# A fused attention and maxout kernel: the pieces ahead of its first loop in another written order

## The chip, the cores and the metric

The kernel runs on 1 core of a Trainium2 chip (8 cores in all). The metric is device time in microseconds of one launch, the median of several runs. Profiled executions give, besides, the span of the kernel's own instructions and the time of each of them.

## The reference

```python
# x: (8, 8, 512, 64), state: (8, 8, 32, 64); per batch b and head h:
scores  = x @ state.T / 8;   a  = softmax(scores,  -1);  xread = a  @ state   # 512 rows
scores2 = state @ x.T / 8;   a2 = softmax(scores2, -1);  sread = a2 @ x       # 32 rows
# heads side by side: 8 * (512 + 32) = 4352 rows of 512
h1 = rows @ w1;  h2 = rows @ w2          # (512, 1024) each
out = maximum(h1, h2) @ w_out            # w_out (1024, 512); float32 out
```

## The kernel before

The kernel uses maximum(h1, h2) = relu(rows @ (w1 - w2)) + rows @ w2. So a first layer with the difference `wd` of the two weights, a relu (`r`), and a second layer with `w_out` (`wo`) give one part. The other part is linear, and for it the product `w2 @ w_out` (`wwo`, 512x512) is made once. Since the rows of a batch are a small softmax matrix times 32 states per head, state times `wd` and state times `wwo` are folded into `sw` (per batch), and `at` (the transposed softmax matrix) is multiplied with `sw`.

The work is staged by batch. Batches 2 to 6 are finished by a loop written at the end of the function, batch 7 by a tail. Batches 0 and 1, the making of `wd`, `wo` and `wwo`, and the first steps of batches 2 to 4 lie ahead of the loop. What is recorded there, and in which order, stands in one string, `ORDER`, of short tokens. Each token calls one helper, so its place sets the place of that helper's instructions in the queue of their engine. Nothing is reordered afterwards: every engine takes its own queue strictly from the front, and waits at the front for what it needs.

A token is read so: name and arguments, then `@` the PSUM banks that it writes, or `>` the engine that does it (A is ScalarE, V is VectorE, P is GpSimd). The ones that matter here:

- `ldx.b.g`, `ldS`, `ldw1.k`, `ldw2.k`, `ldwo.q`: loads from HBM, 512 KB each except the small first `ldS`. They are issued on SyncE (the first `ldS` on ScalarE), and each waits only for the landing of a load further ahead, eight semaphores in turn. The pieces of `w_out` come in the order 2, 3, 0, 1, so `ldwo.3` is the second.
- `ce` casts x (tile `xe`), `xt` transposes it on TensorE (L249), `xte` copies it out of PSUM; `cS`, `S`, `Se` do the same for the state into `sbd`. `sc`, `exp`, `red`, `mul` are the scores and the softmax (`e`, `a`), `at` its transpose on TensorE (L291) and `ate` the copy. `srw` and `swre` make the state read of a batch.
- `cw2.k` casts a quarter of w2, `w2.k` transposes it on TensorE (L548), `w2e.k` copies it to `w2m`. `cwo.q` casts a quarter of w_out into `wo`.
- `ww.i.q` adds the quarter q of `w_out` to `wwo`'s block i: two matmuls 128x512 (L606). `ww.i.q` needs `cwo.q`. `wwe` copies the finished block.
- `sub.k.h` makes a half quarter of `wd` (L560); `sw.b.z` multiplies state with it (L352), `swe` casts the result out of PSUM; `l1.b.f` is the first layer (L375) and `re.b.f` its relu.
- `p1` to `p7`, `k`, `v`, `rs`, `wt`, `dif` are the second layer of batches 0 and 1 (a Strassen-like scheme of seven products, 8 matmuls 128x256 each, L426); `mS` and `Sd` mask the later batches' state and transpose it by DMA into `sbd` (L222, L228).
- `fill.k@bank` is one matmul of a zero tile `wz` with itself into a bank (L575): 256 columns wide, or 512 where k is 100 or more. Its result is never read. There are 27 of them.

```python
    for tok in ORDER.split():                       # L645
        name, _, at_ = tok.partition("@")
        name, _, eng = name.partition(">")
        ...
        if w[0] in mms:
            done[name] = mms[w[0]](*arg)
```

Of the kernel before, what the change touches and what calls it, by code (L numbers as in the profile page):

```python
# [20 lines left out]
CHUNKS = [[(0, 512), (512, 1024)], [(0, 512), (512, 1024)]]  # L21

ORDER = """
ldx.0.0 ldS.0.2 fill.10@0 ldx.0.1 fill.109@1 ldx.1.1 fill.114@0 fill.11@1 ldx.1.0 fill.110@0 ldw2.2 fill.100@1
fill.9@0 ldw2.3 fill.111@1 ldwo.2 fill.0@0 fill.5@1 fill.101@0 ldw1.3 ce.0.1>A ce.0.0>V ldwo.3 xt.0.0@0 cS.0.2>V
ldw1.2 fill.106@1 xte.0.0>V fill.105@2 ce.0.3>P ce.0.2>A ldw2.1 S.0.2@1 xt.0.1@2 ldw2.0 Se.0.2.1>A Se.0.2.0>V sc.0.0@1
xte.0.1>V fill.13@0 ldwo.0 fill.6@3 ce.1.2>P exp.0.0>A fill.115@4 fill.108@3 sc.0.1@4 ce.1.3>V ldwo.1 red.0.0>V
exp.0.1>A xt.1.1@3 ce.1.0>A ce.1.1>P srw.0@4,1 xte.1.1>V ldw1.0 mul.0.0>P swre.0.0>A red.0.1>V sc.1.1@3 xt.1.0@2
cw2.2>P exp.1.1>A ldw1.1 fill.15@4 fill.107@0 xte.1.0>V fill.1@4 swre.0.1>A fill.2@3 fill.14@0 fill.3@4 fill.112@3
cw2.3>A red.1.1>V mul.0.1>P fill.102@4 fill.7@3 ldx.2.0 fill.4@2 mul.1.1>V w2.3@2 cwo.2>A w2.2@3 w2e.3>V sc.1.0@4  # L30
at.0.0@0 at.0.1@1 exp.1.0>A w2e.2>V ww.3.2@2 ldx.2.1 ww.2.2@4 red.1.0>V sub.3.1>P ate.0.0>A srw.1@3,5 ate.0.1>A
mul.1.0>V cwo.3>A ww.0.2@1 sub.3.0>V at.1.0@0 at.1.1@6 swre.1.0>A ww.1.2@7 sub.2.0>V ate.1.1>A ldS.2.8 ww.3.3@2
ww.1.3@7 sub.2.1>V ate.1.0>A ww.0.3@1 swre.1.1>A sw.1.1@0,6 sw.0.1@5,3 swe.1.1.0>A swe.1.1.1>V ww.2.3@4 swe.0.1.0>A
swe.0.1.1>V l1.1.5@6 cw2.1>P srp.0>P srp.1>P l1.1.7@0 cw2.0>A re.1.5>V l1.0.7@3 w2.1@5 re.1.7>V re.0.7>A w2.0@6 w2e.1>V cwo.0>A
l1.0.5@3 l1.1.6@0 w2e.0>V l1.1.4@5 cwo.1>A ww.2.0@4 re.0.5>V ww.1.0@7 re.1.4>A ww.2.1@4 sub.0.0>V ww.1.1@7 re.1.6>A
sub.0.1>V ww.3.0@2 wwe.2>A ww.0.1@1 sub.1.1>V ww.3.1@2 wwe.1>A ww.0.0@1 sub.1.0>V wwe.3>A l1.0.4@7 wwe.0>A cb.2.0>P
sw.0.0@2,4 re.0.4>V wt.0>P sw.1.0@0,5 swe.0.0.0>A swe.0.0.1>V sw.0.w@1,3 sw.1.w@7,6 cb.2.1>P swe.1.0.0>A swe.1.0.1>V xtd.2 wt.1>P
p2.1@2 l1.0.6@4 swe.0.w.0>A re.0.6>V l1.0.3@0 l1.0.2@5 swe.0.w.1>A re.0.3>V swe.1.w.0>V mS.1>A
l1.0.1@4 l1.0.0@1 p2.0@3 swe.1.w.1>V mS.0>A Sd dif.0>P re.0.2>V re.0.1>A re.0.0>A p2o.0
l1.1.0@7 l1.1.1@6 l1.1.2@0 l1.1.3@5 re.1.0>V re.1.1>A re.1.2>A rs.0.0>V rs.0.1>V re.1.3>A  # L40
p2o.1 ldx.4.1 ldx.3.0 ldx.4.0 ldx.3.1
p1.0@1 k0.0>A p1.1@4 rs.0.2>V wt.2>V v00.0 p6.0 rs.0.3>V k0.1>A k1.0>A p5.0@7 wt.3>V v00.1 rs.1.0>V k2.0>A
sc.2.0@6 exp.2.0>A sc.2.1@0 exp.2.1>A sw.2.0@5,3 red.2.0>V mul.2.0>P red.2.1>V swe.2.0.0>A swe.2.0.1>A ce.2.0>A ce.2.1>A ce.2.2>A ce.2.3>A
p7.0 o7.0 v11.0 rs.1.1>V mul.2.1>P p3.0 o3.0 rs.1.2>V atd.2 sw.2.w@6,2 swe.2.w.0>A v01.0 swe.2.w.1>A
p4.0 o4.0 rs.1.3>V ce.3.0>P ce.3.1>P cb.3.0>P ce.3.2>P ce.3.3>P cb.3.1>P v10.0>A store.0 xtd.3 dif.1>P
sr.2@0 p6.1 k1.1>A sw.2.1@5,3 sre.2>V swe.2.1.0>A swe.2.1.1>V p5.1@7 k2.1>A
p7.1 o7.1 v11.1 p3.1 o3.1 v01.1 srt.2@0 srte.2>A p4.1 o4.1 v10.1>A ldx.5.0 ldx.5.1
"""

LATE = 2  # L50
# [851 lines left out]
```

## Time and profile before

| | |
|---|---|
| time of 3 runs | 144.94, 145.07, 145.07 us, median 145.07 |
| the profiled execution | 144.88 us, of which the kernel's span is 143.1 us |
| busy in the span | PE (TensorE) 94%, DVE (VectorE) 76%, ACT (ScalarE) 61%, POOL (GpSimd) 50% |
| HBM | 15.20 MB read, 8.91 MB written |
| granted TensorE clock | 0.996, mean over the span |

The profiled execution is 0.19 us below the median of the runs. The 1.8 us between its time and its span lie outside the instructions. In the profile's rows, PE is a matmul and PEld a weight load, L606 is line 606 of the kernel before, and a name such as `wo<-big` says which tile is written from which. A matmul's duration contains a tail in which the next one already runs, so the pace of a group is read from the chain that ended last, where such tails do not count twice.

### The profile page before, as it was taken

How to read it: one execution, taken by the hardware profiler on the slowest of the kernel's cores; microseconds unless marked ns; L12 is line 12 of the kernel's file. 1: busy time of each engine (PE TensorE's matmuls, PEld its weight loads, DVE VectorE, ACT ScalarE, POOL GpSimd, SP SyncE). 2: the span in 40 equal slices, each digit the busy share in tenths (PEclk: the TensorE clock that was granted, in tenths of full speed). 3: DMA queues.
4: the chain of work that ended last, by engine and by line, in shares of the span. 5: the costliest groups of instructions: out<-in, count | busy, mean ns of one | idle time of the engine just before them, and what ended most of it. 6: DMA issues, size and time to landing. Idle time of an engine off the chain costs nothing.

```text
span 143.1 us, 3680 instructions
## 1 busy us (share of the span) xinstructions
PE 134.7 (94%) x1448; PEld 95.4 (67%) x1458; DVE 108.3 (76%) x197; ACT 86.9 (61%) x168; POOL 72.1 (50%) x99
## 2 busy tenths in 40 slices
PE   6889989999999999999999999999999999999980
PEld 2467725456787776786778477747876786788860
DVE  3488959868999938997899799669948997847420
ACT  4367589895689535855682769086726855753220
POOL 4147326099009993399269908971990464200000
PEclk9999999999999999999999999999999999999998
DMA  3999999945997979949995999759137042502073
GB/s 112 342 366 392 384 386 386 343 83 93 196 343 230 286 180 249 236 42 293 242 386 109 212 355 195 160 213 211 35 65 293 2 58 82 234 5 73 9 248 119
DMA packets 36452, 29.50 MB, mean 206 GB/s; under 512 B 22608, under 2 KB 32336, under 8 KB 35536
## 3 DMA queue, kind: packets, MB, share of 16 engines
q1 hardware_dynamic: 36160, 29.10, 70.8%
q8 instruction: 12, 0.20, 0.6%
q10 hardware_dynamic: 272, 0.13, 0.3%
q14 instruction: 8, 0.07, 0.1%
HBM read 15.20 MB, written 8.91 MB: 169 GB/s over the span
## 4 chain that ended last, share of the span: by engine, by line
PE 83%; DMA 11%; ACT 1%; issue 1%; DVE 0%; SPq 0%; DVEq 0%
PE bank L426 36%; PE bank L375 19%; PE bank L432 10%; DMA big<-in_moe_w_out_dram 8%; PE bank L352 5%; DMA big<-in_x_dram 4%; PE bank L606 3%; PE bank L473 2%; PE bank L515 2%; PE bank L264 2%; PE bank L304 2%; PE bank L513 1%; ACT wo L102 1%; PE bank L548 1%; PE bank L336 0%
## 5 line engine op out<-in xcount | busy, mean ns | idle before, releaser
L102 ACT COPY big<-bank 128x512 f32<-128x512 f32 (+2 forms) x40 | 21.9, 551 | 16.6 <-PE bank L426 8.4
L280 POOL TENSOR_TENSOR a<-e,er 128x512 bf16<-128x512 bf16 x14 | 16.7, 1209 | 29.5 <-ACT e L272 18.0
L370 DVE TENSOR_SCALAR r<-bank 128x512 bf16<-128x512 f32 x32 | 21.9, 690 | 11.7 <-PE bank L375 10.6
L375 PE MATMUL bank<-at,sw 128*128 128x512 bf16 x120 | 29.1, 379 | 0.6 <-DVE sw L104 0.2
L426 PEld LDWEIGHTS <-big 128*128 128x128 bf16 x256 | 23.9, 98 | 6.3 <-DVE er L277 2.1
L426 PE MATMUL bank<-big,big 128*128 128x256 bf16 x192 | 23.1, 273 | 0.1
L102 ACT CAST sw<-bank 128x512 bf16<-128x512 f32 x36 | 20.1, 608 | 3.2 <-PE bank L352 3.2
L375 PEld LDWEIGHTS <-sw 128*128 128x128 bf16 x128 | 12.2, 98 | 13.5 <-ACT sw L102 0.5
L368 ACT ACTIVATE r<-bank 128x512 bf16<-128x512 f32 x32 | 18.3, 597 | 4.9 <-PE bank L375 4.7
L426 PEld LDWEIGHTS <-r 128*128 128x128 bf16 x192 | 18.2, 98 | 3.8 <-issue 0.5
L402 DVE TENSOR_TENSOR big<-bank,big 128x512 f32<-128x512 f32 (+1 forms) x25 | 16.4, 660 | 5.4 <-PE bank L432 5.4
L106 POOL CAST xe<-big 128x512 bf16<-128x512 f32 x23 | 16.5, 749 | 6.1 <-DMA big<-in_x_dram 6.1
L426 PE MATMUL bank<-wo,r 128*128 128x256 bf16 x128 | 16.3, 273 | 0.0
L102 ACT COPY sread_t<-bank 128x128 bf16<-128x128 bf16 x8 | 3.2, 472 | 18.7 <-PE bank L336 15.5
L106 POOL CAST xb<-big 128x1024 bf16<-128x1024 f32 x12 | 12.2, 1035 | 4.7 <-DMA big<-in_x_dram 4.7
L432 PE MATMUL bank<-sw,at 128*128 128x256 bf16 x96 | 14.4, 273 | 0.0
L432 PEld LDWEIGHTS <-at 128*128 128x128 bf16 x128 | 12.5, 98 | 1.7
L402 DVE TENSOR_TENSOR big<-r 128x1024 bf16<-128x1024 bf16 x16 | 12.6, 788 | 0.6
L276 DVE TENSOR_REDUCE sums<-e 128x16 f32<-128x512 bf16 x16 | 10.6, 660 | 0.3 <-ACT e L272 0.2
L272 ACT ACTIVATE e<-bank 128x512 bf16<-128x512 f32 x16 | 8.9, 601 | 1.3 <-PE bank L264 1.3
L402 POOL TENSOR_TENSOR big<-sw 128x512 bf16<-128x512 bf16 x8 | 9.2, 1151 | 0.9 <-POOL a L280 0.9
L104 DVE CAST sw<-bank 128x512 bf16<-128x512 f32 x12 | 7.9, 679 | 0.6 <-PE bank L352 0.6
(100 smaller groups left out, 188.7 us busy)
## 6 DMA issues: line engine op xcount, KB each, us to landing
big<-in_x_dram SPq DMA_DIRECT2D x14, 512.0 KB, 6.2
out_dram<-big SPq DMA_DIRECT2D x7, 1024.0 KB, 5.3
big<-in_moe_w_dram SPq DMA_DIRECT2D x8, 512.0 KB, 12.0
big<-in_moe_w_out_dram SPq DMA_DIRECT2D x4, 512.0 KB, 11.6
big<-in_x_dram SPq DMA_DIRECT2D x1, 1024.0 KB, 6.9
out_dram<-big SPq DMA_DIRECT2D x4, 256.0 KB, 2.6
sf<-in_state_dram SPq DMA_DIRECT2D x1, 384.0 KB, 10.4
out_dram<-w2m SPq DMA_DIRECT2D x2, 128.0 KB, 2.5
```

The costliest lines, as they stand in the source:

```text
L102: nc.scalar.copy(o, i)
L104: nc.vector.tensor_copy(o, i)
L106: nc.gpsimd.tensor_copy(o, i)
L272: nc.scalar.activation(out=e_view(e_s[b % 2], hh).rearrange("p (g c) i n -> p g c (i n)", g=2), in_=p.rearrange("p (c g m) -> p g c m", c= ...
L276: nc.vector.tensor_reduce(es_all[:, b, hh], e_view(e_s[b % 2], hh), axis=AXX, op=ALU.add)
L280: (nc.gpsimd if eng == "P" else nc.vector).tensor_mul(e_view(a_s[b % 2], hh), e_view(e_s[b % 2], hh), er_s[b % 2][:, hh].unsqueeze(3).to_b ...
L368: nc.scalar.activation(out=o, in_=p, func=ACTF.Relu)
L370: nc.vector.tensor_scalar(o, p, scalar1=0.0, scalar2=None, op0=ALU.max)
L375: nc.tensor.matmul(p, sw_s[b % 3][:, g, f * 128:(f + 1) * 128], at_s[b % 3][:, g].rearrange("p c t -> p (c t)"), start=(g == 0), stop=(g = ...
L402: (nc.gpsimd if eng == "P" else nc.vector).tensor_tensor(o, i0, i1, op=op)
L426: nc.tensor.matmul(pv[c], lhs[:, f, 128 * c:128 * c + 128], rhs[:, f, :], start=first and f == 0 and (c == 0 or pv.split), stop=False, ski ...
L432: nc.tensor.matmul(pv[c], at_s[b % 3][:, g, 2 * i + c, :], rhs[:, g, :], start=False, stop=False, skip_group_check=True)
```

## The change

Only the string `ORDER` is another one, and it is one line shorter, so that every later line has a number one lower (L606 is L605 in the kernel after). The tokens of the loads stand in the same order; the number of zero products is the same, 27; the loop and the tail are the same. Other than that nearly every token up to the first instructions of batch 2 has another place, and several have another engine or bank. First and last of it:

```diff
 ORDER = """
-ldx.0.0 ldS.0.2 fill.10@0 ldx.0.1 fill.109@1 ldx.1.1 fill.114@0 fill.11@1 ldx.1.0 fill.110@0 ldw2.2 fill.100@1
...
+fill.115@3 fill.10@6 fill.15@3 fill.100@7 fill.114@5 fill.1@2 fill.107@0 fill.112@4 fill.108@0 fill.9@5 fill.111@3
+fill.106@2 fill.5@7 ldx.0.0 ce.0.1>P ldS.0.2 cS.0.2>P ce.0.0>A fill.105@2 S.0.2@4 Se.0.2.1>V ldx.0.1 ce.0.2>V ce.0.3>A
...
```

Thirteen zero products (8 of 512 columns, 5 of 256) stand ahead of TensorE's first real work, where 11 stood before (6 and 5).

The first place is TensorE's queue around the first product that needs the piece `ldwo.3`. In the kernel before, with the rows that only repeat left out:

```order
L606 MATMUL bank_65<-wo_77,w2m_80 128x512
...
L606 MATMUL bank_67<-wo_77,w2m_80 128x512
...
L606 MATMUL bank_64<-wo_77,w2m_80 128x512
...
L291 MATMUL bank_63<-ident_71,a_94 128x128
...
L291 MATMUL bank_69<-ident_71,a_94 128x128
...
L606 MATMUL bank_70<-wo_77,w2m_80 128x512
...
L606 MATMUL bank_65<-wo_77,w2m_80 128x512
...
L352 MATMUL bank_63<-wd_75,sbd_74 32x512
```

These are `ww.3.2`, `ww.2.2`, `ww.0.2`, `at.1.0`, `at.1.1`, `ww.1.2`, then `ww.3.3`, the first that needs `ldwo.3` (with `ww.1.3` and `ww.0.3` behind it), and `sw.1.1`. The same engine and place in the kernel after:

```order
L605 MATMUL bank_64<-wo_77,w2m_80 128x512
...
L605 MATMUL bank_70<-wo_77,w2m_80 128x512
...
L574 MATMUL bank_63<-wz_73 128x256
...
L290 MATMUL bank_69<-ident_71,a_94 128x128
...
L605 MATMUL bank_64<-wo_77,w2m_80 128x512
...
L605 MATMUL bank_65<-wo_77,w2m_80 128x512
...
L605 MATMUL bank_67<-wo_77,w2m_80 128x512
...
L290 MATMUL bank_66<-ident_71,a_94 128x128
...
L605 MATMUL bank_65<-wo_77,w2m_80 128x512
...
L351 MATMUL bank_63<-wd_75,sbd_74 32x512
```

These are `ww.0.2`, `ww.1.2`, a zero product, `at.1.0`, then `ww.0.3`, now the first that needs `ldwo.3`, and behind it `ww.3.2`, `ww.2.2`, `at.1.1`, `ww.3.3` (and `ww.1.3`), `sw.1.1`. So `ww.3.2`, `ww.2.2` and `at.1.1` (4 matmuls 128x512 and 4 transposes) moved from ahead of that product to behind it.

The second place is ScalarE's queue around the casts of `w_out`. Before:

```order
L102 CAST wo_77<-big_115 128x1024
L272 ACTIVATE e_92<-bank_67 128x8x64
L102 COPY at_99<-bank_63 128x512
L102 COPY at_99<-bank_64 128x512
L102 CAST wo_77<-big_115 128x1024
L102 COPY big_116<-bank_66 128x260
L102 COPY at_100<-bank_69 128x512
```

After:

```order
L271 ACTIVATE e_92<-bank_63 128x8x64
L101 COPY w2m_80<-bank_67 128x4x256
L101 CAST wo_77<-big_115 128x1024
L101 COPY big_116<-bank_69 128x260
L101 CAST wo_77<-big_115 128x1024
L101 COPY at_99<-bank_65 128x512
L101 COPY at_100<-bank_66 128x512
```

The first cast of each fence is `cwo.2`, the second `cwo.3`. The copy `ate.0.1` out of bank 2 (`bank_65`) moved behind `cwo.3`, and `w2e.2` (`w2m`) came onto ScalarE ahead of `cwo.2`.

The third place is ScalarE's queue around the mask of the later batches' state. Before:

```order
L102 CAST sw_102<-bank_64 128x512
L102 CAST sw_102<-bank_66 128x512
L222 ACTIVATE sb_82<-sf_81,mask_83 128x12x64 x2
L368 ACTIVATE r_105<-bank_67 128x512
L368 ACTIVATE r_105<-bank_64 128x512
```

After:

```order
L101 CAST sw_102<-bank_64 128x512
L367 ACTIVATE r_105<-bank_67 128x512
L367 ACTIVATE r_105<-bank_63 128x512
L367 ACTIVATE r_105<-bank_70 128x512
L367 ACTIVATE r_105<-bank_66 128x512
L221 ACTIVATE sb_82<-sf_81,mask_83 128x12x64
```

One of the two masks (`mS.0`) moved behind four relus; the other (`mS.1`) went to GpSimd.

More of the change, by code (lines that the diff above doesn't have):

```diff
@@ L23 @@
 ORDER = """
-ldx.0.0 ldS.0.2 fill.10@0 ldx.0.1 fill.109@1 ldx.1.1 fill.114@0 fill.11@1 ldx.1.0 fill.110@0 ldw2.2 fill.100@1
[L25 to L44, printed above, removed]
@@ L45 @@
-p4.0 o4.0 rs.1.3>V ce.3.0>P ce.3.1>P cb.3.0>P ce.3.2>P ce.3.3>P cb.3.1>P v10.0>A store.0 xtd.3 dif.1>P
-sr.2@0 p6.1 k1.1>A sw.2.1@5,3 sre.2>V swe.2.1.0>A swe.2.1.1>V p5.1@7 k2.1>A
-p7.1 o7.1 v11.1 p3.1 o3.1 v01.1 srt.2@0 srte.2>A p4.1 o4.1 v10.1>A ldx.5.0 ldx.5.1
+fill.115@3 fill.10@6 fill.15@3 fill.100@7 fill.114@5 fill.1@2 fill.107@0 fill.112@4 fill.108@0 fill.9@5 fill.111@3
+fill.106@2 fill.5@7 ldx.0.0 ce.0.1>P ldS.0.2 cS.0.2>P ce.0.0>A fill.105@2 S.0.2@4 Se.0.2.1>V ldx.0.1 ce.0.2>V ce.0.3>A
@@ new lines @@
+ldx.1.1 ldx.1.0 ce.1.0>P ce.1.1>P ldw2.2 ldw2.3 ldwo.2 ldw1.3 ldwo.3 ldw1.2 ldw2.1 ldw2.0 ldwo.0 ldwo.1 ldw1.0 ldw1.1
+ce.1.2>A xt.0.0@5 xte.0.0>V fill.0@2 xt.0.1@1 fill.7@5 fill.3@0 Se.0.2.0>V fill.14@0 sc.0.0@6 ce.1.3>V xte.0.1>V
+fill.110@4 xt.1.1@7 fill.101@1 sc.0.1@4 fill.4@3 fill.13@0 exp.0.0>A red.0.0>V mul.0.0>P xte.1.1>V fill.11@3
+fill.109@6 exp.0.1>A red.0.1>V cw2.2>P cw2.3>V xt.1.0@1 xte.1.0>A srw.0@6,0 swre.0.1>A fill.2@4 sc.1.1@5 exp.1.1>A
+red.1.1>V sc.1.0@0 exp.1.0>A fill.102@5 w2.2@4 mul.0.1>P srw.1@5,0 at.0.0@7 red.1.0>V mul.1.0>V ate.0.0>V swre.1.1>V
@@ new lines @@
+w2e.2>A at.0.1@2 w2.3@4 w2e.3>V cwo.2>A ww.0.2@1 ww.1.2@7 fill.6@0 swre.0.0>A mul.1.1>P at.1.0@6 cwo.3>A ate.0.1>A
+ww.0.3@1 ldx.2.0 ldx.2.1 ldS.2.8 ww.3.2@2 ww.2.2@4 at.1.1@3 ww.3.3@2 ww.1.3@7 ate.1.1>A ate.1.0>V swre.1.0>V sub.2.0>V
+sub.2.1>V sub.3.1>P sub.3.0>P sw.1.1@0,6 swe.1.1.0>A sw.0.1@5,3 ww.2.3@4 swe.1.1.1>V l1.1.7@0 re.1.7>V l1.1.5@6
+swe.0.1.0>A swe.0.1.1>A re.1.5>A cw2.1>P cw2.0>P w2.1@5 w2e.1>V l1.0.7@3 re.0.7>A cwo.0>P w2.0@0 l1.1.4@6 re.1.4>V
+cwo.1>V w2e.0>A l1.1.6@5 ww.2.0@4 l1.0.5@3 re.0.5>A ww.3.0@2 re.1.6>A ww.1.1@7 ww.2.1@4 wwe.2>A ww.1.0@7 ww.3.1@2
@@ new lines @@
+wwe.1>A wwe.3>A wt.0>V sub.0.0>V sub.0.1>V ww.0.0@1 ww.0.1@1 wwe.0>A l1.0.4@6 sub.1.1>V sub.1.0>V sw.0.0@2,4
+swe.0.0.0>A sw.1.0@0,5 swe.1.0.0>A swe.1.0.1>A sw.0.w@1,3 re.0.4>V sw.1.w@7,6 swe.0.0.1>V p2.1@2 l1.0.6@4 l1.0.3@0
+swe.0.w.0>A swe.1.w.1>V re.0.6>A re.0.3>A swe.1.w.0>V swe.0.w.1>V l1.0.1@1 l1.0.0@7 wt.1>V dif.0>V re.0.1>V re.0.0>A
+l1.1.3@5 l1.0.2@3 re.0.2>A mS.0>A wt.2>V rs.0.2>V srp.1>P cb.2.0>P cb.2.1>P ldx.4.1 xtd.2 mS.1>P Sd ldx.3.0 ldx.4.0
+ldx.3.1 l1.1.2@6 l1.1.1@7 re.1.1>A re.1.2>V rs.0.0>V wt.3>V rs.0.1>V p1.0@1 l1.1.0@0 p2.0@3 p2o.0 p5.0@7 re.1.3>A
@@ new lines @@
+re.1.0>A p1.1@4 srp.0>A k0.0>A p6.0 p2o.1 rs.1.0>V v00.0 k0.1>A rs.0.3>V v00.1 k1.0>A sc.2.0@6 exp.2.0>A k2.0>A
+sc.2.1@0 exp.2.1>A sw.2.0@5,3 red.2.0>V mul.2.0>P red.2.1>V swe.2.0.0>A swe.2.0.1>A ce.2.0>A ce.2.1>A ce.2.2>A
+ce.2.3>A p7.0 o7.0 v11.0 rs.1.1>V mul.2.1>P p3.0 o3.0 rs.1.2>V atd.2 sw.2.w@6,2 swe.2.w.0>A v01.0 swe.2.w.1>A p4.0
+o4.0 rs.1.3>V ce.3.0>P ce.3.1>P cb.3.0>P ce.3.2>P ce.3.3>P cb.3.1>P v10.0>A store.0 xtd.3 dif.1>P sr.2@0 p6.1 k1.1>A
+sw.2.1@5,3 sre.2>V swe.2.1.0>A swe.2.1.1>V p5.1@7 k2.1>A p7.1 o7.1 v11.1 p3.1 o3.1 v01.1 srt.2@0 srte.2>A p4.1 o4.1
@@ L48 @@
+v10.1>A ldx.5.0 ldx.5.1
 """
```

## The prediction

> **What bounds the kernel now.** I read the page first, then the chain that ended last, then the timeline at the places where the chain leaves TensorE.
>
> ```profile
> PE 134.7 (94%) x1448; PEld 95.4 (67%) x1458; DVE 108.3 (76%) x197; ACT 86.9 (61%) x168; POOL 72.1 (50%) x99
> PE   6889989999999999999999999999999999999980
> DMA  3999999945997979949995999759137042502073
> PE 83%; DMA 11%; ACT 1%; issue 1%; DVE 0%; SPq 0%; DVEq 0%
> q8 instruction: 12, 0.20, 0.6%
> ```
>
> The second line cuts the span into 40 slices of 3.6 us: TensorE has free tenths in the first six and the last two slices only. The third line says that the DMA engines are full at that time too. The chain has 11% of DMA, and in order of time it shows where.
>
> ```profile
> 6.55 11.23 DMA big<-in_moe_w_out_dram
> 17.79 0.02 issue
> 17.81 1.05 ACT wo L102
> 18.86 0.04 issue
> 18.91 1.46 PE bank L606 x6
> ...
> 23.12 0.89 PE bank L548 x16
> ...
> 25.31 3.45 PE bank L606 x16
> ...
> 37.95 0.87 PE bank L426 x8
> 38.82 0.06 issue
> ```
>
> So what precedes 17.8 us on TensorE does not set the end: the chain goes through the load `ldwo.3`, issued at 6.55 and landed at 17.78, its cast on ScalarE, and the first product that reads it at 18.91. From there to the tail TensorE works with hardly a hole, so work or a wait that is added to it behind 18.91 comes out at the end at full length. The timeline tells what TensorE does around that point.
>
> ```profile
> 17.73 0.59 PE L606 MATMUL bank<-wo,w2m 128*128 128x512 bf16 x2
> 18.91 1.46 PE L606 MATMUL bank<-wo,w2m 128*128 128x512 bf16 x6 [0.58 <-ACT wo L102]
> 20.29 0.67 PE L352 MATMUL bank<-wd,sbd 64*32 64x512 bf16 x16
> 20.89 0.60 PE L606 MATMUL bank<-wo,w2m 128*128 128x512 bf16 x2
> 21.66 0.59 PE L375 MATMUL bank<-at,sw 128*128 128x512 bf16 x2 [0.17 <-DVE sw L104]
> 18.99 1.29 DVE L560 TENSOR_TENSOR wd<-big,big 128x512 bf16<-128x512 f32 x2 [1.22 <-DMA big<-in_moe_w_dram]
> 19.03 1.08 ACT L102 COPY at<-bank 128x512 bf16<-128x512 bf16 x2
> 38.85 1.66 PEld L426 LDWEIGHTS <-big 128*128 128x128 bf16 x16 [0.32 <-DVE big L402]
> ```
>
> The bracket is the idle time and what ended it. Behind 18.91 the holes are 0.17 to 0.3 at 21.66 (the first layer waits for `sw`) and 0.32 at 38.85 (a second-layer product waits for VectorE).
>
> **The change: the first 17.8 us.** Zero products, transposes, casts and the softmax of batches 0 and 1 are in another order there. I cost all of it at nothing, because the load covers it, if TensorE and ScalarE still reach the `ldwo.3` work in time. The rows that limit this:
>
> ```profile
> 9.72 0.61 POOL L106 CAST xe<-big 128x512 bf16<-128x512 f32 x1 [0.88 <-DMA big<-in_x_dram]
> 11.23 0.38 ACT L102 COPY big<-bank 128x260 f32<-128x260 f32 x1 [0.61 <-PE bank L321]
> 11.52 0.60 ACT L272 ACTIVATE e<-bank 128x512 bf16<-128x512 f32 x1
> 12.40 1.05 ACT L102 CAST wb<-big 128x1024 bf16<-128x1024 f32 x1
> ```
>
> The last piece of x lands at 9.7. After, GpSimd casts both its parts, 2 x 0.61, to 10.95; four transposes end near 11.4. Then ScalarE has a row of its own: the copy `xte.1.0` (128x1024 on ScalarE out of PSUM, which the trace doesn't show; between the 0.69 that VectorE takes for it and the 1.05 of the cast, I take 1.05), a state-read copy 0.38, two exponentials 2 x 0.60 with about 0.2 between, `w2e.2` 1.05 and `cwo.2` 1.05, in all to 16.3 or 16.4. A last copy of 0.38 makes it 16.75, and the cast of `ldwo.3` can't begin before 17.8. On TensorE `ww.0.2`, `ww.1.2`, a zero product and `at.1.0` follow `cwo.2`: 0.86 + 0.11 + 0.22, done near 17.6 against 18.9. Both covers have about 1.1 us to spare; an error below that costs nothing, one above it costs its excess. For the same reason 13 zero products ahead of the first transposes where 11 were, a later first score, or a clock that rises earlier or later change nothing.
>
> The loads stand in the same order and wait only for earlier landings, so the landings up to 31 us should be those of before. On SyncE `ldx.4.1` now stands ahead of the DMA transposes and waits for the last subtractions on VectorE; the queue waits there until some 30.3 us and the transposes still go earlier than the 32.9 of before.
>
> **The change: behind the wait.** Both kernels start again at 18.91, but not with the same work left. `ww.3.2`, `ww.2.2` and `at.1.1` were done in the cover of the load and now stand behind `ww.0.3`. A product of 512 columns goes at 3.45 / 16 = 0.216, a transpose at 0.89 / 16 = 0.056 (chain rows above).
>
> - 4 products: +0.86; 4 transposes: +0.22.
> - `ww.3.2` writes bank 2, which ScalarE's copy `ate.0.1` frees, and that copy now stands behind the cast `cwo.3`. The cast begins at 17.81, the next instruction started 0.95 later in before, a copy of this size takes about 0.6 (two in 1.08, overlapped), so the bank is free at 19.36, when `ww.0.3` ends: +0.05. Bounds: 0 and 0.2.
> - `sw.1.1` thus starts at 18.91 + 10 x 0.216 + 0.22 + 0.05 = 21.34 instead of 20.29: +1.05. Its other condition, the subtractions on VectorE (18.99 + 1.29 = 20.28), held it in before for 0.09, and is past now.
> - From `sw.1.1` to the first layer: 21.66 - 20.29 = 1.37 in before, ruled by the eviction of `sw`, with the same tokens between. Unchanged.
> - Later holes that a late TensorE no longer has: 0.32 at 38.85 and bits below 0.1 elsewhere. Bounds: 0 and 0.4 given back. I take 0.3, since the wait is for VectorE, whose queue gets shorter (three relus, an `sw` cast and a `w2m` copy go to ScalarE, two weight sums, a cast and a difference come to it).
> - GpSimd gives two weight sums to VectorE and takes the casts `cw2.0` and `cwo.0`, 1.04 each by the row below, in a stretch where it sat idle for 4 us before the first of its two pieces landed. Their readers, the transposes `w2.0` and the products with that piece, come 1 us later than before. Nothing.
>
> ```profile
> 20.47 1.04 POOL L106 CAST wb<-big 128x1024 bf16<-128x1024 f32 x1 [4.04 <-DMA big<-in_moe_w_dram]
> ```
>
>
> Sum: 1.05 - 0.3 = +0.75; with the bounds of the terms, +0.65 to +1.25. The loop and the tail are the same and have no hole of this size to take it up. The profiled execution is 144.88, so it would be 145.63; on the median of the runs, which is 0.19 higher, 145.07 + 0.75 = 145.8. A measurement of this kernel can tell about 0.2% (0.29 us) from no change.
>
> **The rivals.** *The load lands earlier (faster).* The landing at 17.78 is itself late:
>
> ```profile
> 13.75 1.04 ACT L102 CAST wo<-big 128x1024 bf16<-128x1024 f32 x1 [0.30 <-DMA big<-in_moe_w_out_dram]
> 15.16 1.27 POOL L560 TENSOR_TENSOR wd<-big,big 128x512 bf16<-128x512 f32 x1 [1.73 <-DMA big<-in_moe_w_dram]
> q8 instruction: 1, 0.02, 6.5%
> ```
>
> The first two are readers that wait for pieces landing one after the other, the third is the cast at 17.81 of the chain above: 1.41 apart, then 2.65. The last row is of the DMA view of 15 to 16 us: one packet of instructions, 6.5% of 16 engines for 1 us, so 1.04 us of one engine, and a load is complete when its slowest engine is. This would be TensorE's own next block of instructions, called for when it is so far in its queue. If the changed kernel calls for it over 0.9 us later, `ldwo.3` would land near 16.5, ScalarE would cast it from 16.75, TensorE would go on at 17.85 and be ready for `sw.1.1` at 20.3, as before; with the 0.3 given back, 144.75. Against it: in both programs the same number of instructions (about 260) stands ahead of a point that TensorE passes at 15.5 in before and, by the rows above, between 15.3 and 16.3 now. The Trainium skill, "Runtime: NRT & Kernel Launch", section "Instruction fetch mechanics", has such refills come in 16 KiB blocks of 256 instructions and calls their cost mostly hidden. By that rule the landing would not depend on it and this rival would have no chance; the gap of 2.65 speaks against the rule. Chance 14%.
>
> *The hole is taken up later.* If VectorE and ScalarE are ahead of TensorE by more than I see, and the 0.17 to 0.3 at 21.66 goes as well, the loss is 1.05 - 0.4 - 0.3: 145.4, at the edge of what can be told from no change. Chance 10%.
>
> *The state transpose becomes late.* The third place in the order:
>
> ```profile
> 35.04 1.84 SPq L228 DMA_TRANSPOSE sbd<-sb  x1
> sbd<-sb SPq DMA_TRANSPOSE x1, 4.6
> xt<-xb SPq DMA_TRANSPOSE x6, 5.3
> 40.63 0.63 PE L264 MATMUL bank<-sbd,xt 128*128 128x64 bf16 x16
> 31.52 1.77 ACT L222 ACTIVATE sb<-sf,mask 128x768 bf16<-128x768 f32 x2
> 33.20 1.09 ACT L368 ACTIVATE r<-bank 128x512 bf16<-128x512 f32 x2
> ```
>
> It landed at 39.6, 1.0 ahead of its reader. After, its mask follows the relu of `l1.0.2`, from whose end to the reader TensorE has 3 first-layer blocks (1.29), 5 products of 8 matmuls (4.37) and 8 small matmuls (0.87): 6.5. The path is the tail 0.2, relu 0.55, mask 0.89, transfer 4.6: 6.2. So 0.3 is left. At the 5.3 of a larger transpose (`xt`) it would be 0.4 short: 146.2 to 146.3. Chance 8%.
>
> *The clock falls.* TensorE's hole ahead of 18.91 grows from 0.6 to some 1.3 us.
>
> ```profile
> 1.29 3.81 PE L575 MATMUL bank<-wz 128*128 128x256 bf16 x11 [1.29 <-DVE ones L578]
> 7.23 0.62 PE L249 MATMUL bank<-ident,xe 128*128 128x128 bf16 x8 [0.77 <-ACT xe L102]
> 9.32 0.61 PE L249 MATMUL bank<-ident,xe 128*128 128x128 bf16 x8
> ```
>
> The first 11 zero products (4352 columns) took 0.88 ns a column, twice the 0.42 of later ones: a cold start, 3.8 us long. After the hole of 0.77 eight transposes took 0.62, as those with no hole (0.61). A new cold start would cost half of 3.8, 1.9: 147.7. The Trainium skill, "TensorE: Matmul & The Clock Gate", section "What's actually happening", wants an idle window of about 3.4 us for that. By that rule the hole is too short; the row at 7.23 agrees as far as it goes. Chance 2%.
>
> **How the numbers follow.** Likeliest, 66%: +0.75, 145.8, its own range 145.4 to 146.2. Early load 14%, taken up 10%, late transpose 8%, clock 2%. Faster by over 0.2% (below 144.78): most of the early load, 0.09. Within 0.2% (to 145.36): its rest, 0.05, and half of the taken up, 0.05. Slower: the others, 0.81. The range of 8 in 10 leaves out the early load and the clock, 16%: 145.1 to 146.3.
>
> **What the next profile would show.** Right: the cast of the second `w_out` piece begins again near 17.8; TensorE's hole ahead of 18.9 is over 1 us; behind it ten products of 512 columns and four transposes in place of six, `sw` near 21.3, the first layer near 22.7; no hole at 38.9. Wrong: that cast begins before 17 us, or a new wait for `wo` or `wd` between 21 and 31 us, or the reader of `sbd` near 41.4 waits for a DMA.

## The result and the profile after

The changed kernel takes 146.34 us (median of 6 runs, 145.78 to 146.89), the kernel before beside it 145.00 (6 runs). The ratio is 1.0091 with a 95% interval of 1.0069 to 1.0114: slower by 1.34 us. Forecast was slower by 0.75, at 145.8, with a range up to 146.3. So the sign was right, the size was not, and the time lies just outside the range.

The profiled execution of after is the slowest of its six: 146.89, span 145.0. First the lines of its page: busy times, TensorE's tenths in 40 slices, the chain that ended last, and the queue that brings blocks of instructions.

```profile
PE 135.6 (94%) x1458; PEld 95.5 (66%) x1458; DVE 107.8 (74%) x198; ACT 86.6 (60%) x168; POOL 74.0 (51%) x98
PE   6788869989999999999999999999999999999980
PE 71%; DMA 3%; DVE 2%; ACT 2%; issue 1%; DVEq 0%
q8 instruction: 12, 0.20, 0.6%
```

The totals hardly differ from before. What is new is a 2% of VectorE in the chain (before: 0%), and the 3% of DMA is not the load of before, but a transpose in the loop. The timeline shows the first two of three places; the columns are start, length, engine, line, operation, tiles, count, and in the bracket the idle time ahead and what ended it.

```profile
17.47 0.39 PE L290 MATMUL bank<-ident,a 128*128 128x128 bf16 x4
18.27 1.04 ACT L101 CAST wo<-big 128x1024 bf16<-128x1024 f32 x1 [1.54 <-DMA big<-in_moe_w_out_dram]
19.37 1.51 PE L605 MATMUL bank<-wo,w2m 128*128 128x512 bf16 x6 [1.51 <-ACT wo L101]
20.71 0.39 PE L290 MATMUL bank<-ident,a 128*128 128x128 bf16 x4
20.93 1.03 PE L605 MATMUL bank<-wo,w2m 128*128 128x512 bf16 x4
21.89 0.63 PE L351 MATMUL bank<-wd,sbd 64*32 64x512 bf16 x16
23.01 0.82 PE L374 MATMUL bank<-at,sw 128*128 128x512 bf16 x3
...
30.48 0.40 PE L351 MATMUL bank<-wd,sbd 64*32 64x512 bf16 x4
31.21 0.61 PE L351 MATMUL bank<-wd,sbd 64*32 64x512 bf16 x12 [0.34 <-DVE wd L559]
```

Three places differ. At 19.37 the idle time ahead of the first product with the second piece of `w_out` is 1.51 instead of 0.58, and ten products and four transposes follow it where six products stood; `sw.1.1` starts at 21.89, before at 20.29. And at 31.21 the folding of `wd` for batch 0 (`sw.0.0`) stops in its middle for VectorE. That wait is not in the profile of before, whose row at this place runs through:

```profile
29.12 0.63 PE L352 MATMUL bank<-wd,sbd 64*32 64x512 bf16 x16
```

The chain of after, followed back, starts just ahead of that wait:

```profile
27.22 0.06 DVE big L401
...
27.83 3.34 DVE wd L559 x4
31.17 0.04 issue
31.21 1.04 PE bank L351 x28
...
38.08 0.87 PE bank L425 x8
38.95 0.44 PE bank L431 x4
```

Four subtractions take 3.34 us; in before they took 2.61, and TensorE did not wait for them. At 38.9 the hole of before (0.32, "<-DVE big L402") is gone: two pieces follow each other without a gap.

The third place is in the loop, where the chain goes through a DMA transpose of the softmax matrix (`at<-a`):

```profile
103.92 4.08 DMA at<-a
108.04 3.61 PE bank L374 x16
```

This first-layer group starts 13.60 behind the one at 94.44; in before the same two, at 92.78 and 106.08, are 13.30 apart, and the transpose took 3.4. So 0.30 is lost there, in a loop whose text is the same.

### The profile page after: what moved, and what is told of

Read it like the earlier page. It is cut to its first block, busy times and chain, and to the rows that moved or that the text cites. A ratio compares the mean times of both kernels' runs of the same rounds, so it can differ in the third digit from the quotient of the medians.

```text
span 145.0 us, 3690 instructions
## 1 busy us (share of the span) xinstructions
PE 135.6 (94%) x1458; PEld 95.5 (66%) x1458; DVE 107.8 (74%) x198; ACT 86.6 (60%) x168; POOL 74.0 (51%) x98
## 4 chain that ended last, share of the span: by engine, by line
PE 71%; DMA 3%; DVE 2%; ACT 2%; issue 1%; DVEq 0%
PE bank L425 32%; PE bank L374 17%; PE bank L431 9%; PE bank L351 4%; DMA at<-a 3%; PE bank L472 2%; DVE wd L559 2%; PE bank L514 2%; PE bank L263 2%; PE bank L303 1%; PE bank L512 1%; ACT sw L101 1%; ACT big L101 1%; PE bank L335 0%; ACT w2m L101 0%
## 5 line engine op out<-in xcount | busy, mean ns | idle before, releaser
L279 POOL TENSOR_TENSOR a<-e,er 128x512 bf16<-128x512 bf16 x15 | 18.2, 1228 | 33.2 <-ACT e L271 18.3
L101 ACT COPY big<-bank 128x512 f32<-128x512 f32 (+2 forms) x38 | 21.1, 560 | 15.1 <-PE bank L425 7.1
L374 PE MATMUL bank<-at,sw 128*128 128x512 bf16 x128 | 29.8, 379 | 0.1
L369 DVE TENSOR_SCALAR r<-bank 128x512 bf16<-128x512 f32 x29 | 20.0, 691 | 11.1 <-PE bank L374 10.8
L367 ACT ACTIVATE r<-bank 128x512 bf16<-128x512 f32 x35 | 20.1, 597 | 4.9 <-PE bank L374 4.7
L101 ACT COPY sread_t<-bank 128x128 bf16<-128x128 bf16 x8 | 3.3, 473 | 18.7 <-PE bank L335 15.5
L605 PE MATMUL bank<-wo,w2m 128*128 128x512 bf16 x32 | 7.9, 379 | 1.8 <-ACT wo L101 1.8
L574 PE MATMUL bank<-wz 128*128 128x256 bf16 (+1 forms) x27 | 7.4, 395 | 1.5 <-DVE ones L577 1.3
```

Source lines behind the costliest of these rows:

```text
L101: nc.scalar.copy(o, i)
L279: (nc.gpsimd if eng == "P" else nc.vector).tensor_mul(e_view(a_s[b % 2], hh), e_view(e_s[b % 2], hh), er_s[b % 2][:, hh].unsqueeze(3).to_b ...
L367: nc.scalar.activation(out=o, in_=p, func=ACTF.Relu)
L369: nc.vector.tensor_scalar(o, p, scalar1=0.0, scalar2=None, op0=ALU.max)
L374: nc.tensor.matmul(p, sw_s[b % 3][:, g, f * 128:(f + 1) * 128], at_s[b % 3][:, g].rearrange("p c t -> p (c t)"), start=(g == 0), stop=(g = ...
L605: nc.tensor.matmul(p, w2t[:, f, i, :], wo[:, f, :], start=(first and f % 2 == 0), stop=(last and f % 2 == 1))
```

## The experiments

Two theories. The first: the prediction's step, four products and four transposes behind the load instead of in its cover, is the whole loss, and it is larger than I had it. The second: the step is as large as I had it, and the rest is the new wait at 31.2, made by VectorE's and GpSimd's queues.

### The swap undone: e1_back

The kernel after, with the copy `ate.0.1` ahead of the cast `cwo.3` again, and the four products and four transposes ahead of `ww.0.3`. The diffs from here on show the tokens that move, gathered from their places, not whole lines of the string:

```diff
+ate.0.1>A
 cwo.3>A
-ate.0.1>A
+ww.3.2@2 ww.2.2@4 at.1.1@3
 ww.0.3@1 ldx.2.0 ldx.2.1 ldS.2.8
-ww.3.2@2 ww.2.2@4 at.1.1@3
 ww.3.3@2
```

> The kernel after with three pieces back ahead of the first product that needs the second w_out piece: ww.3.2, ww.2.2, at.1.1, and the copy ate.0.1 ahead of the cast cwo.3. Theory (work that stood under the load's cover stands behind it): TensorE restarts at the same distance from the landing, but sw.1.1 comes about 1.0 us earlier, held then by the subtractions of wd; the wait of 0.5 for wd at 31.2 stays or grows, since VectorE's queue ahead of it ends with a load. In all 0.6 to 1.0 below the kernel after: 145.4 to 145.7. Rival (the loads themselves land later because of the new first microseconds): the landing stays half a microsecond later than in the kernel before and the time stays above 146.0.

Measured: 144.78 (12 runs), ratio to before 0.9994 (0.9973 to 1.0015). The whole loss is gone, more than the 145.4 to 145.7 expected, and the wait for `wd`, expected to stay, is gone too. The rest of the large change cannot be told from nothing. Its timeline:

```profile
18.76 1.46 PE L605 MATMUL bank<-wo,w2m 128*128 128x512 bf16 x6
20.15 0.83 PE L351 MATMUL bank<-wd,sbd 64*32 64x512 bf16 x16
26.30 2.49 DVE L559 TENSOR_TENSOR wd<-big,big 128x512 bf16<-128x512 f32 x4
28.92 0.63 PE L351 MATMUL bank<-wd,sbd 64*32 64x512 bf16 x16
52.05 2.54 PE L374 MATMUL bank<-at,sw 128*128 128x512 bf16 x11
```

TensorE no longer waits at 18.8, nor for `wd`, and reaches the loop's first-layer product at 52.05 (before 52.56, after 54.21). So the swap decides, but this does not yet say by which way: without it the subtractions are also early, end at 28.79, and take 2.49.

### VectorE's queue: e2_wt and e3_both

In the kernel after, VectorE makes a cast of `w_out` (`cwo.1`) and a weight sum (`wt.0`) ahead of the four subtractions; its timeline:

```profile
25.84 0.69 DVE L369 TENSOR_SCALAR r<-bank 128x512 bf16<-128x512 f32 x1 [0.55 <-PE bank L374]
26.45 0.68 DVE L103 CAST wo<-big 128x1024 bf16<-128x1024 f32 x1
27.22 0.69 DVE L401 TENSOR_TENSOR big<-wo 128x1024 bf16<-128x1024 bf16 x1
```

The relu ahead of them waits for TensorE, so a late TensorE makes all of this late. e2_wt has the sum behind the subtractions, and keeps the swap; e3_both has this and the edit of e1_back.

```diff
-wt.0>V
 sub.0.0>V sub.0.1>V
 ...
 sub.1.1>V sub.1.0>V
+wt.0>V
```

> The kernel after with one token moved: the weight sum wt.0 on VectorE behind the four subtractions sub.0.0 to sub.1.0 instead of ahead of them. Theory (VectorE's queue makes sw.0.0 wait): the holes of 0.5 and 0.2 at 31.2 to 32.3 go, 0.5 to 0.7 below the kernel after: 145.7 to 145.8. Rival (TensorE's lateness there is all from the work behind the load, the hole only moves to the first reader of wt.0): no change, 146.3.

> Both edits of the two runs beside it on the kernel after. Theory (two separate losses): the gains add up to 1.1 to 1.5 and the time is that of the kernel before, 145.0 to 145.2. Rival (a third part comes from late landings): 145.4 to 145.7, with the cast of the second w_out piece beginning near 18.3 and not 17.8.

Measured: e2_wt 145.89 (6 runs), ratio 1.0073 (1.0051 to 1.0095); e3_both 144.81 (11 runs), ratio 0.9993 (0.9978 to 1.0008). So by the medians the sum's place is worth 146.34 - 145.89 = 0.45 where the swap is in, and nothing where it is not (144.78 and 144.81). The times alone do not settle the 0.45: the intervals of after and e2_wt overlap (1.0069 to 1.0114, 1.0051 to 1.0095). The traces do: from the start of `sw.0.0` to the second-layer product behind it after has 1.80 (30.48 to 32.28), e2_wt 1.20 (30.06 to 31.26), as before (29.12 to 30.32). The swap alone is worth 145.89 - 144.81 = 1.08, from two kernels that differ in nothing else. The timeline of e2_wt shows the swap without the second wait:

```profile
18.95 1.51 PE L605 MATMUL bank<-wo,w2m 128*128 128x512 bf16 x6 [1.09 <-ACT wo L101]
21.48 0.63 PE L351 MATMUL bank<-wd,sbd 64*32 64x512 bf16 x16
30.06 0.62 PE L351 MATMUL bank<-wd,sbd 64*32 64x512 bf16 x16
53.20 1.46 PE L374 MATMUL bank<-at,sw 128*128 128x512 bf16 x6
```

### GpSimd held back: e5_gate

Why did four subtractions take 3.34? The view of their line, and that of GpSimd's casts of the next batch (columns: shortest, median and longest in ns, then first and last start). In after:

```profile
L559 DVE TENSOR_TENSOR wd<-big,big x4: 684/684/1525, 27.8 to 29.6; 128x512 bf16<-128x512 f32 x4
L105 POOL CAST xb<-big x2: 1232/1240/1247, 29.4 to 30.8; 128x1024 bf16<-128x1024 f32 x2
```

In before:

```profile
L560 DVE TENSOR_TENSOR wd<-big,big x4: 684/688/693, 25.8 to 27.8; 128x512 bf16<-128x512 f32 x4
L106 POOL CAST xb<-big x2: 1035/1036/1037, 28.8 to 31.8; 128x1024 bf16<-128x1024 f32 x2
```

Three subtractions are as long as ever; the fourth, started at 29.6, takes 1.53, 0.84 more. GpSimd's cast had started at 29.4 and ends at 30.6; the subtraction ends 0.5 behind it. In before the last subtraction starts 1.0 ahead of the cast and ends ahead of it. GpSimd's two casts are longer too, 1.23 and 1.25 where before has 1.04; each starts while a subtraction runs. So the suspicion is that the two engines do not read SBUF side by side here. In e5_gate VectorE's queue and the swap stay, and GpSimd alone waits, by a copy of one column of `wd`, until the last subtraction is done:

```diff
 srp.1>P
+gate.1.0>P
 cb.2.0>P cb.2.1>P
```

> The kernel after with one more instruction: GpSimd copies one element of the last half of wd ahead of the two casts cb.2.0 and cb.2.1, so these begin only when VectorE's four subtractions are over. VectorE's own queue stays as it is, with the cast cwo.1 and the weight sum wt.0 ahead of the subtractions. Theory (the subtractions are slow because GpSimd's casts run beside them): they take 2.5 in all instead of 3.3, the hole of 0.5 in front of sw.0.0's later products goes, 0.4 to 0.5 below the kernel after: 145.8 to 145.9. Rival (the queue's order alone makes them late): they still end too late, and the time stays at 146.2 to 146.4.

Measured: 145.86 (6 runs), ratio 1.0076 (1.0053 to 1.0098), the time of e2_wt, and again with an interval that overlaps that of after. The same view:

```profile
L559 DVE TENSOR_TENSOR wd<-big,big x4: 684/684/686, 27.4 to 29.2; 128x512 bf16<-128x512 f32 x4
```

and the timeline of GpSimd:

```profile
30.04 0.19 POOL L105 COPY gt<-wd 128x1 bf16<-128x1 bf16 x1 [4.46 <-DVE wd L559]
30.16 2.02 POOL L105 CAST xb<-big 128x1024 bf16<-128x1024 f32 x2
```

With the weight sum still ahead of them, the subtractions take 2.49 again (27.42 to 29.91), since the casts begin behind them, and `sw.0.0` runs through: 30.07 to 31.26 is 1.19. A wait put into GpSimd's queue made the kernel 0.48 us faster by the medians. Two edits on different engines, with the overlap of these two pieces of work as the only thing in common, remove the same 0.6 from the traces: the collision is shown as the cause of the wait at 31.2. Its worth in the time of the kernel, 0.45 to 0.48, is less sure. In e2_wt GpSimd is the one that comes second, and the longer one:

```profile
L559 DVE TENSOR_TENSOR wd<-big,big x4: 681/682/683, 26.6 to 28.4; 128x512 bf16<-128x512 f32 x4
L105 POOL CAST xb<-big x2: 1031/1326/1620, 29.0 to 30.6; 128x1024 bf16<-128x1024 f32 x2
```

Its first cast, started at 29.0 while VectorE was in the fourth subtraction and then in the weight sum, took 1.62 instead of 1.03; nobody waits for it. The Trainium skill, "SBUF — State Buffer", section "Who interferes with whom", has a VectorE instruction with two SBUF inputs contend with a GpSimd instruction that reads SBUF, since they share a port pair that is an exclusive lock, and lets the order of issue decide who blocks. The rows 1.53 and 1.62 agree: in each it is the later of the two that is longer, by 0.84 and 0.59. So do the 1.23 and 1.25 above, while those that start clear of the other engine's work keep 0.68 and 1.04.

### Parts of the change put into the kernel before: e4_swap, e8_dve, e6_head

e4_swap is the kernel before with its four products alone moved behind the wait:

```diff
-ww.3.2@2
 ldx.2.1
-ww.2.2@4
 ...
+ww.0.3@1 ww.3.2@2 ww.2.2@4
 ww.3.3@2 ww.1.3@7 sub.2.1>V ate.1.0>A
-ww.0.3@1
```

> The kernel before with only this: ww.3.2 and ww.2.2 (four products 128x512) behind ww.0.3 instead of ahead of the load's wait. Theory: 4 x 0.216 = 0.86 more behind the wait, of which at most 0.3 to 0.5 is taken up by later waits of the kernel before (0.3 at 21.7 and 0.3 at 38.9): 145.5 to 145.9. Rival (the later waits take it all up): within 0.2 of 145.0.

Measured: 145.73 (6 runs), ratio 1.0063 (1.0043 to 1.0083), +0.74.

```profile
18.77 2.32 PE L605 MATMUL bank<-wo,w2m 128*128 128x512 bf16 x10 [0.18 <-ACT wo L101]
21.01 0.62 PE L351 MATMUL bank<-wd,sbd 64*32 64x512 bf16 x16
```

Ten products follow the load, and `sw.1.1` is 0.72 later than in before: four products at 0.216 are 0.86, and this execution's load landed 0.14 earlier. The product step carries over into another kernel at the size that the rows gave it. The later waits took nothing up: TensorE is 0.7 late here, and the hole of before at 38.85 is still 0.32, at 39.55.

e8_dve is the kernel before with after's order on VectorE, a cast and the weight sum ahead of the subtractions:

```diff
-cwo.1>A
+cwo.1>V
 ...
+wt.0>V
 sub.0.0>V
 ...
-wt.0>P
```

> The kernel before with VectorE's queue made as that of the kernel after at one place: the cast cwo.1 and the weight sum wt.0 on VectorE ahead of the four subtractions, the work behind the load as in the kernel before. Theory (the second loss needs the subtractions to run into GpSimd's casts): here TensorE is 1.1 us earlier than in the kernel after and so is VectorE, whose subtractions end about when the first cast begins (28.8): 145.0 to 145.3. Rival (the longer queue alone costs it): 0.4 or more, 145.4 and above.

Measured: 144.99 (11 runs), ratio 0.9998 (0.9985 to 1.0011). Nothing. The queue order alone is harmless, since on an early TensorE the subtractions still win against the cast:

```profile
26.64 2.49 DVE L559 TENSOR_TENSOR wd<-big,big 128x512 bf16<-128x512 f32 x4
28.74 1.28 POOL L105 CAST xb<-big 128x1024 bf16<-128x1024 f32 x1 [4.72 <-DMA big<-in_x_dram]
```

e6_head has after's order up to `cwo.3`, with the products and transposes in the cover, and then the kernel before.

> The kernel before with the first part of the kernel after: all tokens up to the cast cwo.3 in the order, on the engines and in the banks of the kernel after (with ww.3.2, ww.2.2 and at.1.1 still ahead of the load's wait, as before), then the rest in the order of the kernel before. Theory (the first 17.8 us lie under the load's cover): the time is that of the kernel before within 0.3, 144.7 to 145.2. Rival (the new first microseconds cost, or bring, something of their own): 145.4 or more, or below 144.6.

Measured: 145.24 (12 runs, 144.77 to 145.91), ratio 1.0025 (1.0005 to 1.0044); its profiled execution is 144.78, with a span of 143.0 (before 143.1). This lies between the two forecasts. The new head brings nothing; that it costs a little by the median, while e1_back with the same head does not, I can't explain, and the spread of its runs is wider than that of before.

### When the block of instructions comes: e7_nofill, e9_refill, e10_more

The prediction had a rival in which TensorE's next block of instructions comes later and the load earlier. In after it did not come later: the DMA view of 15 to 16 us has

```profile
q8 instruction: 1, 0.02, 6.6%
```

as in before. To move it, e7_nofill drops the last 16 of the 27 zero products of the kernel before, which stand in four lines of the string:

```diff
-fill.106@1 fill.105@2 fill.13@0 fill.6@3 fill.115@4 fill.108@3 fill.15@4 fill.107@0
-fill.1@4 fill.2@3 fill.14@0 fill.3@4 fill.112@3 fill.102@4 fill.7@3 fill.4@2
```

> The kernel before without the last 16 of its 27 zero products (the first 11 stay), which takes 32 instructions out of TensorE's queue. Theory (a load lands a microsecond late because TensorE's next block of instructions is fetched beside it): the fetch moves from 15 us to 17 us or later, the landing of the second w_out piece follows the one ahead of it by 1.4 instead of 2.3 to 2.7, so at 16.4, and the long step shows at a later landing; the time is 0 to 0.4 below the kernel before, since sw.1.1 then waits for the next piece. Rival (the long step belongs to that load, wherever the fetch is): it stays at the ninth landing, and the time stays within 0.3 of 145.0.

Measured: 146.95 (5 runs), ratio 1.0128 (1.0109 to 1.0146), 2 us slower. But the step asked for is there. ScalarE's timeline, and the DMA view of 17 to 19 us:

```profile
16.89 1.07 ACT L99 CAST wo<-big 128x1024 bf16<-128x1024 f32 x1
```

```profile
q8 instruction: 1, 0.02, 3.3%
```

The block came at 17.8 instead of 15.5, and the second piece of `w_out` was there at 16.57 (before 17.79; in the eight other experiments, with the block near 15, 17.51 to 17.84, in after 18.25). The trace has the landing of a load in 16 parts: in before 15 of them were there at 16.45 and the last at 17.79, in e7_nofill all 16 at 16.57, and in e9_refill below, with the block at 17.8 too, all at 16.56. So in these traces a block of instructions in flight costs the load beside it about 1 us, by one part of 16. The Trainium skill, "Runtime: NRT & Kernel Launch", section "Instruction fetch mechanics", calls the cost of such a block mostly hidden; here it shows in a landing. It brought no time: the first layer started at 21.52, the loop's first-layer product at 52.42 (before 52.56), since TensorE lost in front what the load gave. Its clock fell to half; the view by stretches gives the length, the busy time of PE, PEld, DVE, ACT and POOL, the granted clock, the DMA share and GB/s.

```profile
5.20:8.60 3.40, 1.72 (x28) 1.26 (x25) 1.95 (x6) 1.15 (x4) 0.88 (x2) 1.00 1.05 344
8.60:12.00 3.40, 3.35 (x31) 2.71 (x32) 3.00 (x6) 1.86 (x4) 2.54 (x4) 0.50 1.03 379
```

The 2 us went in the loop, where TensorE waited three times for a DMA transpose of the softmax matrix (`at<-a`):

```profile
66.80 1.46 PE L372 MATMUL bank<-at,sw 128*128 128x512 bf16 x5 [0.78 <-DMA at<-a]
94.07 1.24 PE L372 MATMUL bank<-at,sw 128*128 128x512 bf16 x4 [0.32 <-DMA at<-a]
121.62 1.67 PE L372 MATMUL bank<-at,sw 128*128 128x512 bf16 x6 [0.87 <-DMA at<-a]
```

Those three took 4.9, 4.3 and 4.7 us from issue to landing, where before has 3.1 to 3.6. With 16 matmuls and their weight loads fewer, all later blocks are called for elsewhere in the loop. Two kernels for that: e9_refill is e7_nofill with 16 zero products of 32 columns ahead of the first layer, e10_more the kernel before with the same 16 added.

```diff
-            nc.tensor.matmul(p[:, 0:z.shape[1]], z[:, 0:128], z, start=True, stop=True)
+            nc.tensor.matmul(p[:, 0:z.shape[1]], wz[:, 0:128], z, start=True, stop=True)
...
+idle.16.6.32
 l1.1.5@6
```

> The kernel before without the last 16 of its 27 zero products (as in the run e7_nofill, which took 146.95), but with 16 narrow zero products (32 columns) put into TensorE's queue right ahead of the first layer's first product, near 21.2 us, where TensorE waits some 0.3 us anyway. From there on TensorE has as many instructions behind it as in the kernel before, so its later blocks of instructions are called for at the same places of the program as there (near 62.4, 87.4, 115.8 us) instead of 64.7, 90.6, 119.5. Theory (the loss of 2 us in e7_nofill's loop comes from where the blocks' transfers fall against the DMA transposes of the softmax matrix): the transposes take 3.1 to 3.6 us again, no hole of 0.5 to 1 us at them; 16 x 0.029 = 0.46 us of products less the wait of 0.33 are added: 145.0 to 145.6. Rival (the loss comes from something that the missing early products leave behind, the half clock near 10 us or the order of landings): three transposes of 4.3 to 4.9 us as in e7_nofill, 146.9 to 147.4. The block behind 15.5 us still comes after the load of the second piece of w_out (landing near 16.6) by both.

> The kernel before with the same 16 narrow zero products ahead of the first layer's first product, all 27 others kept: its later blocks of instructions are called for 16 products earlier in the program, some 3 us, than before (near 59, 71, 84, 91, 101, 112 us). The price of the 16 products is 16 x 0.029 - 0.33 of wait = 0.1 to 0.5 us, which e9_refill shares. Theory (place of the blocks against the transposes): if none falls 2 to 3 us behind a transpose's issue (issues near 62.2, 75.7, 89.2, 102.5, 115.8), all transposes take 3.1 to 3.6: 145.1 to 145.5; the block near 91 is the one that could cost up to 1 us. Rival (place of the blocks is without effect): 145.1 to 145.5 too, and e9_refill 146.9 or more.

Measured: e9_refill 145.44 (12 runs, 144.62 to 146.82), ratio 1.0024 (0.9994 to 1.0054); e10_more 146.80 (6 runs), ratio 1.0120 (1.0096 to 1.0145). In e9_refill all six transposes are back at 3.1 to 3.6 and no wait for them is left: 16 added products made e7_nofill 1.5 us faster. Its clock fell to 0.50 as well, from 9.89 to 13.31, and its load landed as early, so neither is the cause of the 2 us. e10_more missed the 145.1 to 145.5 that both its theories gave: the same 16 made the kernel before 1.8 us slower, of which their own price is at most 0.5:

```profile
107.72 1.46 PE L374 MATMUL bank<-at,sw 128*128 128x512 bf16 x6 [0.98 <-DMA at<-a]
```

One transpose took 4.9 there, issued at 102.75, with a block at 105.2. So the number of TensorE's instructions ahead of the loop, apart from the work in them, moves this kernel by 1 to 2 us, by way of the transposes: that is shown. That the block which falls into a transpose is what lengthens it is likely and not settled: a block 2.5 us behind the issue went with 4.9 in e10_more, with 4.0 in e1_back and with 3.4 in before, and which of the 16 engines carries what, the trace does not tell.

For the case itself the loop's blocks come at the same places of the program in before and in after (62.4 and 64.1, 87.4 and 89.2, 115.8 and 117.9, while the loop's first-layer product is at 52.56 and 54.21). Yet the transposes have a part in it, the third place above: after, e1_back, e2_wt, e3_both and e5_gate all have one transpose of 4.0 to 4.1, and the groups around it are 13.53 to 13.60 apart, against 13.29 to 13.31 in before, e4_swap, e6_head, e8_dve and e9_refill. So what after has behind `cwo.3` costs 0.23 to 0.30 in the loop, with or without the swap. It is no part of the 1.1 and 0.45, which are differences between kernels that share it. Why this transpose is longer stays open.

## Why the prediction was wrong in size

Step by step, in the prediction's order:

- *The first 17.8 us cost nothing.* Held, as far as the runs tell: e1_back and e3_both carry all of the new head and cannot be told from before; the 0.27 of e6_head stays open. (By after's trace 14 zero products, 9 and 5, stand ahead of the first transposes, not 13.) TensorE and ScalarE were ready in time: the transposes at 17.47 end ahead of the wait, and ScalarE idled 1.54 ahead of the cast. The load landed at 18.25, 0.46 later than in the profile of before, with the same loads in the same order; five experiments with the same head had it at 17.51 to 17.84, so that is this execution's own, and most of the 0.55 by which it lies above its kernel's median.
- *Behind the wait: four products, four transposes, the bank: +1.05.* Held. From 19.37 to `sw.1.1` are 2.52 us, against 1.38 in before: +1.14. In the times of whole kernels the swap is 1.08 (e2_wt against e3_both).
- *From `sw.1.1` to the first layer unchanged.* It became 1.12 instead of 1.37: some 0.25 was given back, as in the rival that I had at 10%, but not by its reason. A late TensorE alone does not shorten it: in e4_swap, with the old order and 0.7 late, it is 1.35 (21.01 to 22.36). So it comes from the new order; which token does it was not tested.
- *0.3 given back at 38.85.* The hole is gone, as forecast, but the lateness of TensorE is not the reason: it is gone in e1_back, where TensorE is early, and stays in e4_swap, where it is late. The new order takes it away. e1_back reaches the loop 0.5 earlier than before: 0.14 from the start of `sw.1.1`, 0.07 up to the first layer, 0.3 here.
- *The loop and the tail are the same.* Their text is, their time is not: the longer transpose takes 0.23 to 0.30 there. That is why of the 0.5 in e1_back only 0.2 shows in the medians (144.78 against 144.99, not told apart from nothing). It is a second, smaller term that was put at nothing. What was given back ahead of the loop, 0.55, less this comes near the 0.3 forecast; that agreement is luck.
- *VectorE's "queue gets shorter", and GpSimd's moved work: "Nothing".* This is the step that failed. VectorE's total did get shorter (108.3 to 107.8), but a wait is ruled by what stands ahead of one instruction, and ahead of the four subtractions a cast and a weight sum had been put, 1.4 us (26.45 to 27.83). Together with a TensorE 1.1 later, whose relus go first in the same queue, the last subtraction came behind the start of a cast on GpSimd whose own start is set by a load, and not by TensorE. Forecast 0, measured 0.6 in the traces, 0.45 (e2_wt) and 0.48 (e5_gate) by the medians.

Sum from the medians: 1.08 for the swap, 0.45 for the collision, 0.19 given back: 1.34. It comes out by construction, since these are the steps from before over e3_both and e2_wt to after; the check is the profiled execution. At the loop's first-layer product: 0.46 landing + 1.14 - 0.25 + 0.6 at 31 - 0.3 at 39 = 1.65, the difference of 54.21 and 52.56. With the 0.3 in the loop that is 1.95, and the spans differ by 145.0 - 143.1 = 1.9. The prediction had 1.05 for the swap, 0.3 given back, and nothing for the rest. (Its bounds add up to +0.60 to +1.20, since the 1.05 holds 0.05 for the bank already; the measured 1.34 is above either.)

The rivals: the load did not land earlier, since the block came at 15.4 as in before; e7_nofill shows that its mechanism exists, and that there it brought no time. The state's transpose took 3.7 and was down at 41.1, ahead of its reader at 42.28. The clock stayed at 1.00 through the hole. And one of the signs named for being wrong, a new wait for `wd` between 21 and 31 us, is what came, just behind that stretch, at 31.2. The kernels without the swap are not measurably faster than before, so no version here beats it.

## What to carry to other kernels

A term costed at "nothing" needs the start times of both neighbours: when one queue is shifted by a microsecond and another engine's work hangs on a load that does not shift, look which instructions now overlap, and whether they share a port. Do not judge a moved instruction by its engine's total, but by what stands ahead of the one instruction that somebody waits for. And when two versions differ in the number of instructions on TensorE, part of their difference can be the place of the instruction blocks: give them equal counts before you read 1% as the work's.

## What the runs showed of the hardware

- VectorE's subtraction of two f32 tiles in SBUF and GpSimd's cast of an f32 tile in SBUF took turns: 0.68 became 1.53 behind a cast that had begun 0.25 earlier, 1.03 became 1.62 behind a subtraction and a sum of two bf16 tiles.
- A block of TensorE's instructions (16 KB, 1.05 us of one DMA engine) made a 512 KB load land about 1 us later; moved from 15.5 to 17.8 us, it left the load at 16.57.
- Sixteen narrow zero products more cost 1.8 us in one kernel and brought 1.5 us in another, through DMA transposes of 3.0 to 3.6 us that became 4.3 to 4.9.
- TensorE's granted clock fell to 0.50 for 3.4 us in e7_nofill behind a stretch of 3.4 us with 1.72 us of TensorE's work in it; the same stretch of the kernel before holds 2.29, and its clock stayed at 1.00. In e9_refill it fell behind a stretch of 3.4 us (6.48 to 9.89) with 1.91 in it; 2.16 in after (18.12 to 21.53) did not make it fall. The Trainium skill, "TensorE: Matmul & The Clock Gate", section "What's actually happening", wants an idle window for the fall; here half a stretch of that length in work did not prevent it.
